# Retention and two feed-forward layers on one core: background work drawn from two queues, upper parts and rectifiers queued apart from what they depend on

## The chip, the core and the metric

The kernel runs on one core of a Trainium2 chip. A core has TensorE (PE in the profile; PEld is its loading of weights), VectorE (DVE), ScalarE (ACT), GpSimd (POOL) and SyncE (SP), each with its own queue that it works through in order, and 16 DMA engines that they share. Here nearly all DMAs are issued from SP's queue. The metric is the time of one execution in device microseconds (us).

## What is computed

```python
# retention, per batch and head, for t in 0..767 (4 batches, 8 heads, head size 64)
state = gamma * state + outer(k[t], v[t])
y[t] = scale * (q[t] @ state)
# y as x: 3072 tokens x 512, then two feed-forward layers, 512 -> 2048 -> 512
h = x @ w_in;   x = maximum(0.01 * h, h) @ w_out
h = x @ w2_in;  out = (h - tanh(h)) @ w2_out
```

Weights come as 64-bit floats and are turned into 32-bit ones on the chip.

## The kernel before

**Stages.** Retention runs first, in 24 steps of one chunk of 128 times and one pair of heads, for all batches. In step `s` TensorE transposes k of step `s+1` and a part of q, computes y of step `s` (after VectorE has put the decay on its scores: the two `A`), the state's update (`u`, not in the last chunk) and the scores of step `s+1`. ScalarE scales k (two instructions of 128x256), copies the transposes (`kT`, `qT`) and y out of PSUM. Then comes the first layer's first matrix product ("the stream" below): blocks of 128x512 by a Strassen-Winograd scheme, 3 superblocks of tokens (`sb`, two chunks of 512 tokens each) times 8 groups of weights (`g`) times 7 products (P1, P2, P5, P6, P3, P7, P4), 168 products of 6 matmuls. Last are the first layer's second product (lines 628 to 654, 96 rounds of 12 matmuls) and the second layer (96 rounds of 24).

**Split precision.** Every operand of a matmul is cut into an upper part (ScalarE rounds it, `xch`, `wgh`, `gh`) and a lower part (VectorE takes the upper part from the source, `xcl`, `wgl`, `gl`), and three matmuls take the place of one. `split` writes both, one behind the other (line 129).

**Order of the stream.** `stream` sorts the products by slot: 56 slots for each superblock, 7 for each group, and an offset from `PROD`: P1 at 0, P2 at 1, P5 at 2, P6 at 4, P3 at 5, P7 at 10, P4 at 13. PSUM banks are X (four, for P1, P6, P7, P4, which add up in one bank), Y (two, P5 and P3 in one bank) and Z (two, P2). After a product `collect` takes its bank: P1, P6 and P5 are copied out by ScalarE (`copy_out`, L563, the tile P); after P2, P3 and P7 VectorE adds a kept copy (`add_up`, L569, the tile c) and ScalarE rectifies that sum at once (`rectify`, L545), and SP stores it to `g1s`; P4 is rectified straight from its bank. P3 may start when the copy of P5 has left bank Y, P6 when the copy of P1 has left X, and P4 when VectorE has read P7's sum from X.

**Background work.** Generators issue the work that prepares operands, and each yields the VectorE time that it has just issued: `conversion` loads a raw block (512 KB), ScalarE takes its absolute value (`s1`, L159), VectorE makes the float in four instructions (`s2`, L163 to L171); `build_wg` makes the operands of a weight group from two converted blocks (sums `s12` and `s34` by VectorE, then `split`); `build_xc` makes those of a superblock of tokens (differences by VectorE, L293, and `split`); `keep_out` splits a converted `w_out` block; `store2` stores a block for the second layer. In the retention two queues run: `conv` from step 4 with 1.3 us a step, `bg` from step 8 with 1.0 us. In the stream there is one queue, `bg`, with 1.3 us a product less 0.7 where VectorE adds; its members run one after the other, and a load is waited for where the next instruction needs it.

**Code names.** The lines that the change and the prediction touch: 118 (`run`), 129, 175, 204, 222, 260, 271, 501 to 518 (retention's loop), 566, 590 to 615 (the stream's loop), 625, 748 to 778.

## Time and profile before

| | us |
|---|---|
| median of 3 runs (1199.52 to 1203.79) | 1202.17 |
| the profiled execution | 1197.38 |
| its span, first to last instruction | 1195.5 |
| retention, up to 118.80 | 118.8 |
| the stream, up to the first matmul of the second product | 286.1 |
| the rest | 790.6 |

In the rows below a line of the timeline begins with its start and its length in us from the span's start; a bracket at its end holds the time that the engine stood idle just before it and what ended that. A line of waits has who waited for whom, the us in total, the number of times and the longest. A group of instructions has its count, then busy us and mean ns of one. The granted clock is a share of full speed; in the rows by stage the DMA columns are the busy share and GB/s.

### The profile page before, as it was taken

Reading aid. Unit: us, or ns where it says so; the run is one execution under the profiler, and the core shown is the slowest. Engines: PE = TensorE matmul, PEld = TensorE weight load, DVE = VectorE, ACT = ScalarE, POOL = GpSimd, SP = SyncE. Lnnn points to the kernel's source line nnn. Section 1 sums busy time; section 2 is a strip of 40 time slices with the busy share of each in tenths; the row PEclk is TensorE's granted clock in tenths of the full one; section 3 lists DMA queues with packets and bytes.
Section 4 is the critical chain, followed back from the end, with each engine's and each line's share of the span. In section 5 each row is a group of like instructions: output and inputs, shape, how many; then the busy total and the mean of one; then the engine's idle time right before and its main releaser. Section 6 shows DMA issues by size and latency. Waiting matters only on the chain.

```text
span 1195.5 us, 16441 instructions
## 1 busy us (share of the span) xinstructions
PE 1146.0 (96%) x6075; PEld 938.3 (78%) x6075; DVE 754.5 (63%) x1264; ACT 592.9 (50%) x1025; POOL 168.6 (14%) x156
## 2 busy tenths in 40 slices
PE   9899888799899699999999999999999999999998
PEld 6788666587677588888888888888888888888886
DVE  3588674682677556544344567776767676767665
ACT  5666554554555424324444454545554544554544
POOL 2231000000000000000000132232232232232221
PEclk9999999999899899999999999999999999999999
DMA  9993464484456668645564100100200100200000
GB/s 230 266 241 92 174 223 141 147 293 177 158 194 211 234 232 311 236 155 214 211 244 136 71 1 1 71 1 1 71 1 2 71 1 1 71 1 1 36 1 36
DMA packets 134448, 148.02 MB, mean 124 GB/s; under 512 B 57440, under 2 KB 86240, under 8 KB 134368
## 3 DMA queue, kind: packets, MB, share of 16 engines
q1 hardware_dynamic: 134080, 146.83, 36.8%
q8 instruction: 47, 0.77, 0.3%
q14 instruction: 33, 0.27, 0.1%
q10 hardware_dynamic: 288, 0.15, 0.0%
HBM read 96.61 MB, written 50.33 MB: 123 GB/s over the span
## 4 chain that ended last, share of the span: by engine, by line
PE 66%; DVE 1%; DMA 0%; issue 0%; ACT 0%; SPq 0%; ACTq 0%
PE o L645 22%; PE acc L711 22%; PE h L697 22%; DVE c L569 0%; DMA gr<-g1s 0%; DMA g1s<-c 0%; DVE cv L168 0%; PE X L556 0%; ACT c L545 0%; ACT wo L132 0%; DVE cv L163 0%; DVE cv L165 0%; DVE wo L133 0%; DVE st L719 0%; ACT gh L132 0%
## 5 line engine op out<-in xcount | busy, mean ns | idle before, releaser
L133 POOL TENSOR_TENSOR gl<-e,gh 128x512 fp32r<-128x512 f32 x95 | 122.9, 1294 | 933.1 <-ACT gh L132 876.9
L645 PE MATMUL o<-gh,wo 128*128 128x512 f32 x768 | 238.5, 392 | 4.9 <-ACT gh L132 4.9
L645 PEld LDWEIGHTS o<-gh,wo 128*128 128x128 f32 x768 | 145.2, 189 | 35.6 <-ACT gh L132 5.6
L132 ACT ACTIVATE gh<-e 128x512 fp32r<-128x512 f32 x96 | 60.7, 633 | 220.2 <-DVE e L738 220.2
L731 DVE SCALAR_TENSOR_TENSOR e<-e,h 128x512 f32<-128x512 f32 x96 | 66.0, 687 | 152.4 <-ACT e L729 152.4
L645 PE MATMUL o<-gl,wo 128*128 128x512 f32 x384 | 150.4, 392 | 0.0
L711 PE MATMUL acc<-w2h,gl 128*128 128x512 f32 x384 | 149.7, 390 | 0.0
L711 PE MATMUL acc<-w2l,gh 128*128 128x512 f32 x384 | 149.5, 389 | 0.0
L711 PE MATMUL acc<-w2h,gh 128*128 128x512 f32 x384 | 149.5, 389 | 0.0
L697 PE MATMUL h<-xkl,w2h 128*128 128x512 f32 x384 | 149.5, 389 | 0.0
L697 PE MATMUL h<-xkh,w2l 128*128 128x512 f32 x384 | 149.5, 389 | 0.0
L697 PE MATMUL h<-xkh,w2h 128*128 128x512 f32 x384 | 149.5, 389 | 0.0
L133 DVE TENSOR_TENSOR gl<-gr,gh 128x512 fp32r<-128x512 f32 x96 | 65.7, 689 | 115.5 <-ACT gh L132 94.7
L132 ACT ACTIVATE gh<-gr 128x512 fp32r<-128x512 f32 x96 | 59.2, 627 | 74.1 <-DMA gr<-g1s 47.7
L545 ACT ACTIVATE c<-c 128x512 f32<-128x512 f32 x72 | 45.5, 632 | 100.9 <-DVE c L569 91.9
L645 PEld LDWEIGHTS o<-gl,wo 128*128 128x128 f32 x384 | 72.6, 189 | 15.6 <-DVE gl L133 0.4
L711 PEld LDWEIGHTS acc<-w2h,gl 128*128 128x128 f32 x384 | 72.1, 188 | 15.7 <-DVE gl L133 0.4
L711 PEld LDWEIGHTS acc<-w2h,gh 128*128 128x128 f32 x384 | 72.1, 188 | 15.0 <-ACT gh L132 0.2
L697 PEld LDWEIGHTS h<-xkh,w2h 128*128 128x128 f32 x384 | 72.1, 188 | 15.0
L697 PEld LDWEIGHTS h<-xkl,w2h 128*128 128x128 f32 x384 | 72.1, 188 | 14.9
L697 PEld LDWEIGHTS h<-xkh,w2l 128*128 128x128 f32 x384 | 72.1, 188 | 14.9
L711 PEld LDWEIGHTS acc<-w2l,gh 128*128 128x128 f32 x384 | 72.1, 188 | 14.9
(99 smaller groups left out, 2002.9 us busy)
## 6 DMA issues: line engine op xcount, KB each, us to landing
g1s<-c SPq DMA_DIRECT2D x96, 256.0 KB, 2.1
gr<-g1s SPq DMA_DIRECT2D x96, 256.0 KB, 5.5
raw<-in_moe_w_in_dram SPq DMA_DIRECT2D x32, 512.0 KB, 5.5
raw<-in_moe_w_out_dram SPq DMA_DIRECT2D x32, 512.0 KB, 4.7
w2s<-cv SPq DMA_DIRECT2D x32, 256.0 KB, 3.4
w2r<-w2s SPq DMA_DIRECT2D x16, 512.0 KB, 5.3
q<-in_q_dram SPq DMA_DIRECT2D x24, 256.0 KB, 4.0
k<-in_k_dram SPq DMA_DIRECT2D x48, 128.0 KB, 3.8
```

The source lines that it names most:

```text
L132: nc.scalar.activation(out=hi, in_=src, func=AF.Copy)
L133: eng.tensor_tensor(out=lo, in0=src, in1=hi.bitcast(F32), op=ALU.subtract)
L545: nc.scalar.activation(out=t, in_=src, func=AF.Prelu, alpha=0.01)
L645: nc.tensor.matmul(ACC[j], a, b, start=m == 0 and i == 0, stop=m == NM - 1 and i == 2)
L697: nc.tensor.matmul(h, a, b, start=kt == 0 and i == 0, stop=kt == NK - 1 and i == 2)
L711: nc.tensor.matmul(ACC[j], a, b, start=m == 0 and i == 0, stop=m == NM - 1 and i == 2)
L731: nc.vector.scalar_tensor_tensor(out=w, in0=u, scalar=C3, in1=h, op0=ALU.mult, op1=ALU.mult)
```

## The change

What it does, part by part:

- **Two queues, one allowance.** `run` takes several queues in order and goes on to the next where one yields None. Retention's loop draws from `conv` and `bg` in turn (odd steps `conv` first, even steps `bg` first), 2.3 us a step from step 5; in the stream the order is `bg`, `bx` (tokens), `conv`.
- **Loads are passed over.** A counter `tick` rises by 3 in a retention step, 1 in a stream slot, 2 in a round of the second product. A conversion's `s1` is issued 5 ticks after its load at the earliest, and the operands loaded for a superblock too.
- **Upper parts apart.** `build_wg` and `build_xc` issue upper parts ahead of the sums or lower parts of the item before. In `build_xc` the differences for T3 and T4 go to GpSimd.
- **Late rectifiers.** `add_up` notes its rectifier in `late`; the loop issues it after the next product's `collect`.
- **Moves.** The whole of `conv_in` is in retention's queue, `w2` blocks ahead of the second product are 8, not 10; the first 5 loads of `gr` are issued in the stream's last 8 slots; `split_g(n + 2)` stands behind `mm_out1(n)`; the second layer's weights may start at round 56, not 64.

```diff
-ATT_UNITS, CONV_FROM, CONV_US = 10, 4, 1.3
-BG_FROM, BG_US = 8, 1.0
+CONV_FROM, ATT_US = 5, 2.3
+LOAD_LEAD = 5
...
-    def run(queue, us):
-        while us > 0 and queue:
-            cost = next(queue[0], "end")
+    def run(queues, us):
+        while us > 0:
+            for queue in queues:
+                cost = next(queue[0], "end") if queue else None
+                if cost is not None:
+                    break
+            if cost is None:
+                return 0.0
...
+        def load(n):
+            if n < last:
+                units[n].load()
+                at[n] = tick[0] + LOAD_LEAD
...
             if n < last:
+                while tick[0] < at[n]:
+                    yield None
                 units[n].s1()
             if 1 <= n <= last:
                 yield from units[n - 1].s2()
+                load(n - 1 + ahead)
...
     def build_wg(g):
...
+        upper(ts[0], a)
         nc.vector.tensor_tensor(out=s12[:, :H2], in0=b[:, :H2], in1=b[:, H2:], op=ALU.add)
-        yield 0.37
+        yield 0.4
         nc.vector.tensor_tensor(out=s12[:, H2:], in0=s12[:, :H2], in1=a[:, :H2], op=ALU.subtract)
-        yield 0.37
...
-        yield pair(a, "A11", "A12")
-        yield pair(s12, "S1", "S2")
+        yield 0.4
+        upper(ts[2], s12)
+        lower(ts[0], ts[1], a)
+        yield 0.7
...
+        upper(ts[4], s34)
+        lower(ts[2], ts[3], s12)
+        yield 0.7
+        upper(w["N22"][0], b[:, H2:], -1.0)
+        lower(ts[4], ts[5], s34)
+        yield 0.7
+        lower(*w["N22"], b[:, H2:], -1.0)
...
     def load_xq(sb, at):
-        while now[0] < at:
+        while now[0] < at or raws[0]:
             yield None
...
+        todo = (("B11", b11, "P1", None), ("B21", b21, "P2", (nc.vector, b11, b12, b11)), ("T1", b11, "P5", None),
+                ("T2", b11, "P6", None), ("B22", b22, "P3", (nc.gpsimd, b12, b22, b12)), ("T3", b12, "P7", None),
+                ("T4", b21, "P4", None))
+        for nm, src, by, nxt in todo[:3] if part == 0 else todo[3:]:
...
+            if nm == "T2":
+                minus(nc.vector, b11, b22, b11)
+            out = [(alloc("xch", F32R), alloc("xcl", F32R)) for _ in range(2)]
             for kt in range(2):
...
+                upper(out[kt][0], src[kt])
+            yield 0.0
+            for kt in range(2):
+                lower(*out[kt], src[kt])
                 yield 0.7
...
+            if nxt:
+                minus(*nxt)
+                yield 1.3 if nxt[0] is nc.vector else 0.0
+            if nm == "T3":
+                minus(nc.gpsimd, b21, b11, b21)
...
+            tick[0] += 3
             if s >= CONV_FROM:
-                c_us = run(conv, c_us + CONV_US)
-            if s >= BG_FROM and s < len(steps) - 1:
-                b_us = run(bg, b_us + BG_US)
+                us = run((conv, bg) if s % 2 else (bg, conv), min(us + ATT_US, ATT_US))
...
-        rectify(sb, g, half_m, half_t, t, t)
+        late.append((sb, g, half_m, half_t, t, t))
...
+        done, late[:] = late[:], []
         used = collect(sb, g, nm)
+        for args in done:
+            rectify(*args)
...
-        if i >= BG_START:
-            us = run(bg, min(us + SLOT_US - used, 2.0))
+        us = run((bg, bx, conv), min(us + SLOT_US - used, SLOT_US))
+        if len(stream) - 8 <= i < len(stream) - 8 + G_AHEAD:
+            load_g(i - len(stream) + 8)
```

Where the instructions stand, at three places. In the names, `x1` is a block of y, `xch` an upper part of a token operand, `cv` a converted block, `wgh` (of the change: `wg`) a part of a weight operand, `c` a sum to be rectified.

**Retention, steps 19 and 20, ScalarE.** Before, from k's scaling in step 19 on:

```order
L382 ACTIVATE k_21_1413<-k_21_1413,lead_65 128x4x64 [waits DMAHW6_49]
L382 ACTIVATE k_21_1413<-k_21_1413,lead_65 128x4x64 [waits DMAHW7_49]
L405 ACTIVATE kT_20_1570<-kTp_20_1565 128x512 [waits PE_49,Activation_49]
L418 ACTIVATE qT_20_1497<-qTp_20_2_1572 128x2x2x128 [waits PE_49]
L464 ACTIVATE x1_50_1595<-y_19_1578 128x512 [waits PE_49]
L132 ACTIVATE xch_51_1613<-x1_2_280 128x512 [waits DVE_49]
L132 ACTIVATE xch_53_1617<-x1_4_409 128x512 [waits DVE_49]
L382 ACTIVATE k_22_1482<-k_22_1482,lead_65 128x4x64 [waits DMAHW4_49]
```

In the change, ScalarE in step 20 and the start of step 21:

```order
L498 ACTIVATE x1_59_1654<-y_20_1637 128x512 [waits PE_49]
L142 ACTIVATE xch_60_1683<-x1_1_201 128x512 [waits DVE_49]
L142 ACTIVATE xch_62_1685<-x1_3_337 128x512 [waits DVE_49]
L142 ACTIVATE xch_64_1691<-x1_6_538 128x512
L142 ACTIVATE xch_66_1693<-x1_8_673 128x512
L416 ACTIVATE k_23_1554<-k_23_1554,lead_65 128x4x64 [waits DMAHW6_49]
L416 ACTIVATE k_23_1554<-k_23_1554,lead_65 128x4x64 [waits DMAHW7_49]
L439 ACTIVATE kT_22_1705<-kTp_22_1700 128x512 [waits PE_49,Activation_49]
L452 ACTIVATE qT_22_1630<-qTp_22_2_1707 128x2x2x128 [waits PE_49]
```

And VectorE at that place in the change: the scores of step 21, then the background of step 20, then the scores of step 22:

```order
L476 SCALAR_TENSOR_TENSOR A_21_0_1676<-sc_21_0_1666,cst_100 128x512 [waits PE_49]
L476 SCALAR_TENSOR_TENSOR A_21_1_1678<-sc_21_1_1667,cst_100 128x512 [waits PE_49]
L150 SCALAR_TENSOR_TENSOR wg_53_1407<-cv_28_1016,wg_53_1407 128x256 [waits Activation_49]
L313 TENSOR_TENSOR x1_1_201<-x1_6_538,x1_1_201 128x512
L313 TENSOR_TENSOR x1_3_337<-x1_8_673,x1_3_337 128x512
L148 TENSOR_TENSOR xcl_61_1684<-x1_1_201,xch_60_1683 128x512 [waits Activation_49]
L148 TENSOR_TENSOR xcl_63_1686<-x1_3_337,xch_62_1685 128x512 [waits Activation_49]
L148 TENSOR_TENSOR xcl_65_1692<-x1_6_538,xch_64_1691 128x512 [waits Activation_49]
L476 SCALAR_TENSOR_TENSOR A_22_0_1742<-sc_22_0_1732,cst_100 128x512 [waits PE_49]
```

In the change the first two upper parts wait for differences that stand on VectorE behind step 21's scores and in the same step; before, the differences that the two upper parts of step 19 read (L293) were VectorE's work of steps 17 and 18, ahead of step 20's scores. In the change k's scaling and `kT` of step 22 stand behind four upper parts.

**The stream, third and fourth group of the first superblock, ScalarE.** Before, from P1's copy of the fourth group to P6's:

```order
L563 ACTIVATE P1_129_2143<-X_0_3_2136 128x512 [waits PE_49]
L159 ACTIVATE cv_130_2147<-raw_6_0_2115 128x512 [waits DMAHW7_49,DMAHW0_49]
L545 ACTIVATE c_131_2158<-c_131_2158 128x512 [waits DVE_49]
L563 ACTIVATE P5_132_2170<-Y_0_3_2163 128x512 [waits PE_49]
L159 ACTIVATE cv_133_2175<-raw_14_0_2119 128x512 [waits DMAHW1_49,DMAHW0_49]
L545 ACTIVATE c_134_2184<-c_134_2184 128x512 [waits DMAHW2_49,DVE_49,Activation_49]
L563 ACTIVATE P6_135_2195<-X_0_3_2136 128x512 [waits PE_49]
```

In the change, the same:

```order
L606 ACTIVATE P1_129_2140<-X_0_3_2133 128x512 [waits PE_49]
L176 ACTIVATE cv_130_2145<-raw_6_0_2045 128x512 [waits DMAHW1_49]
L606 ACTIVATE P5_132_2166<-Y_0_3_2159 128x512 [waits PE_49,Activation_49]
L588 ACTIVATE c_131_2156<-c_131_2156 128x512 [waits DMAHW0_49,DVE_49]
L142 ACTIVATE wg_135_2175<-cv_111_2029 128x512 [waits DMAHW3_49]
L606 ACTIVATE P6_143_2199<-X_0_3_2133 128x512 [waits DMAHW0_49,PE_49]
L588 ACTIVATE c_142_2190<-c_142_2190 128x512 [waits DMAHW6_49,DVE_49]
```

The rectifier of the sum after P2 (`c_131` in both) stood ahead of P5's copy and now stands behind it, and the one after P7 behind P6's copy.

**The end of the stream, SP.** Before, the stream's last three stores and the first loads for the second product (`gr`):

```order
L546 DMA g1s_69<-c_418_4032 128x512 [waits DMAHW3_49,Activation_49]
L546 DMA g1s_69<-c_419_4044 128x512 [waits DMAHW4_49,Activation_49]
L546 DMA g1s_69<-c_420_4055 128x512 [waits DMAHW5_49,Activation_49]
L628 DMA gr_423_4062<-g1s_69 128x512 [waits DMAHW6_49,PE_49]
L628 DMA gr_424_4064<-g1s_69 128x512 [waits DMAHW7_49,PE_49]
L628 DMA gr_425_4066<-g1s_69 128x512 [waits DMAHW0_49,PE_49]
```

In the change:

```order
L568 DMA gr_407_3960<-g1s_69 128x512 [waits DMAHW6_49,PE_49]
L589 DMA g1s_69<-c_404_3952 128x512 [waits DMAHW7_49,Activation_49]
L568 DMA gr_409_3972<-g1s_69 128x512 [waits DMAHW0_49,PE_49]
L568 DMA gr_412_3986<-g1s_69 128x512 [waits DMAHW1_49]
L589 DMA g1s_69<-c_413_3994 128x512 [waits DMAHW2_49,Activation_49]
L589 DMA g1s_69<-c_410_3980 128x512 [waits DMAHW3_49,Activation_49]
L170 DMA raw_15_1_4009<-in_moe_w_out_dram 128x1024 [waits DMAHW4_49,DVE_49]
```

The first five loads of `gr` stood behind the stream's last store and now stand ahead of the last four stores.

## Rows read from the trace of the kernel before

**Rows 1.** By stage: length, busy PE, PEld, DVE, ACT, POOL, granted clock, DMA:

```profile
0.00:118.80 118.80, 113.04 (x1611) 95.21 (x1611) 77.10 (x133) 72.97 (x144) 29.93 (x51) 1.00 0.81 209
118.80:404.89 286.09, 246.44 (x1009) 193.00 (x1008) 181.60 (x324) 153.39 (x278) 0.00 (x0) 0.95 0.53 187
404.89:1195.50 790.61, 786.50 (x3456) 650.11 (x3456) 495.80 (x809) 366.51 (x603) 138.69 (x105) 1.00 0.25 88
```

**Rows 2.** The chain that ended last, a piece of the second product (two rounds):

```profile
663.15 5.44 PE o L645 x24
```

**Rows 3.** What TensorE waited for between 100 and 440 us:

```profile
PE Y L556 <- ACT P L563: 21.7, 12, 4.3
PE X L556 <- DVE c L569: 7.5, 9, 2.5
PE X L556 <- ACT P L563: 2.9, 1, 2.9
PE X L556 <- ACT wgh L132: 2.5, 2, 1.3
```

**Rows 4.** What ScalarE waited for, 110 to 440 us:

```profile
ACT c L545 <- DVE c L569: 91.9, 61, 5.1
ACT cv L159 <- DMA raw<-in_moe_w_in_dram: 11.1, 5, 4.3
```

**Rows 5.** Timeline of the stream at the first superblock's end:

```profile
208.97 0.69 DVE L569 TENSOR_TENSOR c<-Z,P 128x512 f32<-128x512 f32 x1 [3.49 <-DMA g1s<-c]
209.74 0.63 ACT L545 ACTIVATE c<-c 128x512 f32<-128x512 f32 x1 [5.08 <-DVE c L569]
210.80 0.58 ACT L563 ACTIVATE P<-Y 128x512 f32<-128x512 f32 x1
211.43 0.79 PE L556 MATMUL Y<-xch,wgh 128*128 128x512 f32 x1 [3.05 <-ACT P L563]
```

**Rows 6.** Timeline where a conversion meets a load that is not there:

```profile
322.43 0.66 ACT L159 ACTIVATE cv<-raw 128x512 f32<-128x512 f32 x1 [2.89 <-DMA raw<-in_moe_w_out_dram]
325.40 0.79 PE L556 MATMUL Y<-xch,wgh 128*128 128x512 f32 x1 [3.62 <-ACT P L563]
```

**Rows 7.** Timeline at the stream's end:

```profile
398.04 0.50 PE L556 MATMUL X<-xch,wgn 128*128 128x512 f32 x1 [2.49 <-DVE c L569]
404.89 0.79 PE L645 MATMUL o<-gh,wo 128*128 128x512 f32 x1 [4.86 <-ACT gh L132]
```

**Rows 8.** Timeline of retention, steps 4 and 5:

```profile
35.63 0.66 ACT L159 ACTIVATE cv<-raw 128x512 f32<-128x512 f32 x1 [3.94 <-DMA raw<-in_moe_w_in_dram]
38.94 1.23 PE L438 MATMUL sc<-qT,kT 64*128 64x128 f32 x16 [3.07 <-ACT kT L405]
```

**Rows 9.** Timeline of retention between the scores of two steps (84.65 and 89.27):

```profile
84.65 1.16 PE L438 MATMUL sc<-qT,kT 64*128 64x128 f32 x16
85.84 1.29 DVE L442 SCALAR_TENSOR_TENSOR A<-sc,cst 128x512 f32<-128x512 f32 x2 [0.59 <-PE sc L438]
85.88 0.90 ACT L382 ACTIVATE k<-k,lead 128x256 f32<-128x256 f32 x2
86.68 0.58 ACT L405 ACTIVATE kT<-kTp 128x512 f32<-128x512 f32 x1
87.05 0.42 DVE L163 TENSOR_SCALAR cv<-cv 128x512 f32<-128x512 f32 x1
89.27 1.16 PE L438 MATMUL sc<-qT,kT 64*128 64x128 f32 x16
```

**Rows 10.** Timeline of retention's last chunk, scores of two steps that follow each other:

```profile
111.00 1.16 PE L438 MATMUL sc<-qT,kT 64*128 64x128 f32 x16
115.19 1.16 PE L438 MATMUL sc<-qT,kT 64*128 64x128 f32 x16
```

**Rows 11.** Timeline of retention with GpSimd at work beside VectorE:

```profile
87.61 3.41 POOL L394 TENSOR_TENSOR qp<-q,lead 128x256 f32<-128x256 f32 x4 [5.40 <-DMA q<-in_q_dram]
87.96 0.98 DVE L168 SCALAR_TENSOR_TENSOR cv<-raw,cv 128x512 int32<-128x512 int32 x1
```

More of the change, by code (lines that the diff above doesn't have):

```diff
@@ L173, in s2, with conversion @@
             yield 0.75
-    def conversion(units, ahead=RAW_BUFS - 1):
+    def conversion(units, ready=None, ahead=RAW_BUFS - 1):
+        while ready and not ready():
+            yield None
         last = len(units)
-        for u in units[:ahead]:
-            u.load()
+        at = {}
+        raws[0] += 1
+        def load(n):
+            if n < last:
+                units[n].load()
+                at[n] = tick[0] + LOAD_LEAD
+        for n in range(ahead):
+            load(n)
         for n in range(last + 2):
             if n >= 2:
-                cost = units[n - 2].done(units[n - 2])
-                if cost:
-                    yield cost
-            if 0 < n < last and n - 1 + ahead < last:
-                units[n - 1 + ahead].load()
+                yield from units[n - 2].done(units[n - 2])
             if n < last:
+                while tick[0] < at[n]:
+                    yield None
                 units[n].s1()
@@ L205, in keep_out @@
         WO[u.m] = alloc("wo", F32R), alloc("wo", F32R)
-        split(*WO[u.m], u.y, nc.vector)
+        nc.scalar.activation(out=WO[u.m][0], in_=u.y, func=AF.Copy)
+        yield 0.0
+        lower(*WO[u.m], u.y)
         give(u.y)
-        return 0.7
+        yield 0.7
     conv_out = [Convert(moe_w_in, moe_w_out, m, 1, keep_out) for m in range(NM)]
@@ L222, in build_wg @@
     def build_wg(g):
-        while g + NG not in UN or g not in UN:
+        while g + NG not in UN or g not in UN or len(free) < 10:
             yield None
@@ L267, in load_xq, with build_xc @@
             q[nm] = [t[:, 0], t[:, 1]]
+        arrive = tick[0] + LOAD_LEAD
+        yield 0.0
+        while tick[0] < arrive:
+            yield None
         XQ[sb] = q
-        yield 0.01
-    def build_xc(sb, done=None):
+    def build_xc(sb, part, done=None):
         while sb not in XQ:
@@ L542, in get_bank @@
         return BK[sb, g, b], False
+    late = []
     def rectify(sb, g, half_m, half_t, src, t):
@@ L588, in collect, with made @@
         return 0.0
-    bg.extend(conv)
-    bg.extend(build_wg(g) for g in (2, 3, 4))
-    bg.append(conversion(conv_in[ATT_UNITS:]))
-    bg.extend(build_wg(g) for g in range(ATT_UNITS // 2, NG))
-    bg.extend((load_xq(1, 44), build_xc(1), conversion(conv2[:W2_EARLY]), load_xq(2, SPAN + 44), build_xc(2),
-               conversion(conv_out)))
+    def made(sb):
+        return lambda: len(XC.get(sb, ())) == 7
+    conv.extend((conversion(conv2[:W2_EARLY], made(1)),
+                 conversion(conv_out, made(2))))
+    bg.extend(build_wg(g) for g in range(2, NG))
+    bx = deque()
+    for sb in range(1, NSB):
+        bx.extend((load_xq(sb, SPAN * (sb - 1) + 38), build_xc(sb, 0), build_xc(sb, 1)))
     xleft = [(c, p) for c in range(2, NC) for p in range(NPAIR)]
@@ L600 @@
         while g not in WG or bn not in XC.get(sb, {}):
-            now[0] = at_
-            if not bg or run(bg, 0.01) == 0.0:
-                raise RuntimeError(f"{sb} {g} {nm} is not ready")
+            tick[0] += 1
+            run((bg, bx, conv), 0.01)
         product(sb, g, nm)
         now[0] = at_
+        tick[0] += 1
+        done, late[:] = late[:], []
         used = collect(sb, g, nm)
+        for args in done:
+            rectify(*args)
         if sb == NSB - 1 and nm == "P4":
@@ L746, in el_2 @@
         give(gt)
[L748 to L749 removed]
     for n in range(2):
         split_g(n, nc.vector)
[L752 to L753 removed]
+    conv.append(conversion(conv2[W2_EARLY:]))
+    bg = deque([second_weights()])
     us = 0.0
+    first_x = None
     for n in range(NT):
         load_g(n + G_AHEAD)
+        while n % NM not in WO:
+            tick[0] += 1
+            run((conv,), 0.01)
+        mm_out1(n)
         split_g(n + 2, nc.vector)
[L758 to L760 removed]
+        tick[0] += 2
         nb, m = divmod(n, NM)
[L762 to L763 removed]
+        if conv:
+            us = run((conv,), min(us + (W2_US if n >= NM else 1.9), 1.9))
         else:
[L765 removed]
+            if first_x is None:
                 load_x(0)
[L767 to L770 removed]
+                first_x = n
+            if first_x + 3 <= n < first_x + 7:
+                split_x(0, n - first_x - 3, nc.vector)
+            if n >= max(first_x + 7, 3 * NM + 8):
+                us = run((bg,), min(us + 1.3, 1.4))
         k = n - (NT - 4)
@@ L774 @@
             el_1(k // 2)
-    assert not bg
-    while bg2:
-        run(bg2, 1.0)
+    assert not conv
+    while bg:
+        run((bg,), 1.0)
     for n in range(-LAG, NT):
```

113 lines of the change are left out of this document (44 added, 69 removed).

## The prediction

> **What bounds the kernel now.** I read the table by stage first [rows 1]. In the last 790.6 us TensorE is busy for 786.5 at a granted clock of 1.00, its full 2.4 GHz, and two rounds of 12 matmuls take 5.44 us [rows 2], 0.227 us a matmul. The reader is to see that nothing is left there: 3456 matmuls by 0.227 are 783.5 us. In retention TensorE is busy for 113.0 of 118.8 us with small matmuls. The stream is the loose stage: 1008 matmuls by 0.227 are 228.5 us (1.36 us a product, a "slot"), and it took 286.1, so 57.6 us are lost. The second view is what TensorE waited for [rows 3]: 21.7 us for ScalarE's copy before bank Y is used again, 2.9 for the same copy before bank X, 7.5 for VectorE's sum, 2.5 for upper parts of weights, and 4.9 at the end of the stage for the first upper part of the second product [rows 7]. That is 39.5 us of idle time. The other 18.1 are TensorE at work but slow: the granted clock was 0.95 over the stage [rows 1], and it fell from 2.4 GHz towards 1.2 behind the longer gaps.
>
> The third view says why ScalarE's copy is late. ScalarE stood 91.9 us, 61 times, in front of a rectifier whose sum VectorE had not made [rows 4]. One such place in order [rows 5]: VectorE's sum starts at 208.97, the rectifier comes at 209.74 after 5.08 us of idle ScalarE, the copy of bank Y behind it at 210.80, and TensorE starts at 211.43 after 3.05 idle. The copy itself needed only TensorE; it stood in the wrong place in the queue. A second cause has the same look from TensorE: a conversion's absolute value stands in ScalarE's queue until its block has landed (11.1 us for one of the two matrices, at longest 4.3, [rows 4]), and the copy behind it is late: 2.89 idle on ScalarE, then 3.62 on TensorE [rows 6].
>
> **The change part by part: the stream.** Late rectifiers put a rectifier behind the next product's copy, by which time TensorE's next 1.36 us have passed and the sum is normally there. Passing over loads gives a block 5 slots, 6.8 us by 1.36, more than the longest wait of 4.3 [rows 4]. Upper parts issued ahead let VectorE find them ready. By waits [rows 3], what is late next and what stays:
> - Copy before Y, 21.7 us: P3 follows P5 by two slots less its own copy, so the copy may be 2.7 us late. At the two changes of superblock it stands behind four upper parts of about 0.6 each, two of which wait for differences; I leave 0.7 us at each, about 1.5.
> - Copy before X, 2.9: nothing stays. Upper parts of weights, 2.5: 0.3 stays, since the first group is made during retention.
> - VectorE's sum, 7.5 in 9 waits, the last of them 2.49 [rows 7]. P4 follows P7 directly at the very end, where VectorE has four conversion instructions (two of 0.42 [rows 9], two of 0.69, about 2.2) between P3's sum and P7's, while two products pass: about 1.0 stays there, and half of the other 5.0: 3.5.
> - The end, 4.9. The loads of `gr` no longer stand behind the last stores, so their landing is hidden by the last products. What is late next is ScalarE: behind the last product stand P4's rectifier (0.58, like the copy [rows 5]), the late one (0.63 [rows 5]), an absolute value (0.66 [rows 6]) and the first upper part (0.6): 2.4 stays.
>
> So 7.7 us of idle stay of 39.5. The slow work goes with the gaps: 18.1 by 7.7 / 39.5 is 3.5. The stream falls from 57.6 us lost to 11.2, a gain of **46.4**. The bounds: nothing lost at all would be 57.6; if half of the loss stays, 28.8.
>
> **Retention.** The first conversion now waits two steps for its load instead of blocking ScalarE in step 4. That block held ScalarE for 3.94 us and TensorE for 3.07 [rows 8]: gain **3.1**.
>
> The alternation costs something in return. In step s the background stands behind the step's scores on VectorE: of the two `A`, started at 85.84, the next instruction begins at 87.05 [rows 9]. Before, an upper part that needed a difference was issued a step later. Now it stands in the same step (the first of the places shown with the diff), and behind it in ScalarE's queue are k's scaling and `kT`, without which TensorE can't make the next scores. Scaling starts at 85.88, `kT` ends at 87.26, the scores start at 89.27 [rows 9]: 2.0 us to spare, so scaling may start by 87.9. By the order six even steps hold such a wait. With 1.29 us for two VectorE instructions of 128x512 and 0.42 for one of half the width or with one operand [rows 9], and 0.6 for an upper part, scaling starts at
> - step 10, two differences, the second upper part: 87.05 + 1.29 + 0.05 + 0.5 = 88.9, late by 1.0;
> - step 12, a lower part and two half-wide sums: late by 1.2;
> - step 14, two half-wide sums, then an upper part and a half-wide one: 0.9;
> - steps 16 and 18, three and two half-wide ones: 1.0 and 0.9, and 0.46 more each, since in the last chunk the next scores come after 4.19 us instead of 4.62 [rows 9, 10]: 1.4 and 1.4;
> - step 20, a half-wide one, two differences and then four upper parts: 90.4, so 2.5 + 0.46 = 3.0.
>
> Together **8.9** us, all on the path, because TensorE has no slack in this stage. It can be 0 if ScalarE's and VectorE's queues run further ahead than in these rows, or some 15 if each also slows the step behind it. Net cost of retention: 5.8. The extra 0.8 us of allowance a step has cover: VectorE is busy for 77.1 of 118.8 [rows 1].
>
> **GpSimd.** Twelve differences go from VectorE to GpSimd, 12 by 0.65 (half of 1.29 [rows 9]), 7.7 us off VectorE. I cost them at nothing, since VectorE is busy for 181.6 of 286.1 in the stream [rows 1] and TensorE bounds it. But the two engines disturb each other: while GpSimd scaled q for 3.41 us, VectorE's instruction of 128x512 took 0.98 us [rows 11] and not 0.69 [rows 5]. At 0.3 for each difference it is 3.6 us of VectorE time, below what is saved. The Trainium skill (SBUF — State Buffer, "SBUF: two separate sides") is harder on this edit: GpSimd and a VectorE instruction with two SBUF inputs take a shared pair of ports as an exclusive lock, and the loser waits for the whole instruction. By it a difference of about 1.7 us (two of the four in 3.41) could hold VectorE as long, 12 by 1.7 or 20 us, more than the edit saves; the row shows a delay but no full block, and the sum goes by the row.
>
> **Rest.** The second product's first 16 rounds get 1.9 us of background each, with one lower part of 0.69: 2.6 of 2.72 [rows 2], covered as long as TensorE takes 2.72 a round. No change there.
>
> **The sum.** 46.4 + 3.1 - 8.9 = 40.6. Against the profiled execution: 1197.4 - 40.6 = 1156.8. The median of the runs lies 4.8 above that execution, so I forecast 1202.2 - 40.6 = **1161** us (chance 0.55).
>
> **The rivals.**
> - Retention doesn't pay: ScalarE's queue has more slack than the rows say. For it: it is idle for 46 of 118.8 us [rows 1]. Against it: a single late instruction there cost 3.07 [rows 8]. Then 46.4 + 3.1: 1153. Chance 0.2.
> - The change doesn't do what it says about loads: SP works in order, and a load issued behind a store that waits for a rectifier starts late, so that 5 slots are too few. Then the waits for blocks stay, 10.8 us of idle (2.9 [rows 3], 3.6 [rows 6] and the longest, 4.3 [rows 3]) with their share of slow work, by 57.6 / 39.5 is 15.8: 1177. If GpSimd's differences also hold VectorE at the superblocks' changes, up to 1185. Chance 0.17.
> - Slower: the wait that takes the rectifier's place. By the order 29 upper parts in the stream stand behind VectorE's work. If each costs TensorE what it costs in retention, 8.9 / 6 or 1.5 us, that is 43 us idle and with the slow work 63: 1161 + 63 = 1224. It turns the sign from 0.96 us each (40.6 / 29 / 1.46). Against it: in the stream the copy has 2.7 us to spare, in retention the step has 2.0, and TensorE waited only 2.5 us for such parts before [rows 3]. Chance 0.05.
> - Gains and costs within 0.3% of each other: 0.03.
>
> **How the numbers follow.** The likeliest is the sum, 1161. From 1147 (the first rival, less half of the 11.2 us that the sum leaves to the stream) to 1185 lie the forecast, the first rival and most of the second; about 0.15 is left out. A change of 0.3% is about what a measurement of this kernel can tell from none. Faster by more than that: 0.92 (0.55 + 0.2 + 0.17); within: 0.03; slower: 0.05.
>
> **What would show it.** Right: in the profile after, the stream lasts about 240 us, ScalarE's waits for VectorE's sums fall below 15 us, TensorE's wait for the copy before Y nearly goes, the gap ahead of the second product is about 2.4, and the clock over the stream is 0.98 or more. In retention six gaps of 1 to 3 us stand before the scores, with `kT` as what ended them, and no gap at 36; retention ends near 125. Wrong: gaps before Y with a conversion's absolute value or an upper part ahead of the copy, or a last stage with TensorE idle.

## The result

| | before | after |
|---|---|---|
| median of 4 runs, us | 1201.62 (1199.52 to 1203.79) | 1158.25 (1157.96 to 1158.29) |
| the profiled execution, its span | 1197.38, 1195.5 | 1157.96, 1156.2 |
| retention, up to its last matmul | 118.8 | 127.2 |
| the stream, up to the second product | 286.1 | 238.9 |
| the rest | 790.6 | 790.1 |

The ratio is 0.9638, with a 95% interval of 0.9621 to 0.9656: 3.6% faster. The spans differ by 47.2 - 8.4 + 0.5 = 39.3 us. The stages of the changed kernel, as [rows 1]:

```profile
0.00:127.20 127.20, 115.33 (x1611) 96.62 (x1611) 79.70 (x133) 73.16 (x147) 36.21 (x55) 0.99 0.78 201
127.20:366.09 238.89, 232.12 (x1009) 189.81 (x1008) 169.44 (x291) 147.50 (x270) 12.26 (x8) 0.99 0.62 216
366.09:1156.20 790.11, 786.13 (x3456) 649.48 (x3456) 506.07 (x830) 369.95 (x609) 138.78 (x105) 1.00 0.25 90
```

The granted clock of the stream rose from 0.95 to 0.99 (1.00 is 2.4 GHz throughout; below it, a part of the stretch ran at 1.2). What TensorE waited for between 20 and 400 us (total, times, longest), which answers [rows 3]:

```profile
PE sc L472 <- ACT kT L439: 9.6, 6, 2.8
PE o L691 <- ACT gh L137: 2.3, 1, 2.3
PE Y L599 <- ACT xch L142: 2.1, 1, 2.1
PE X L599 <- DVE c L612: 1.0, 1, 1.0
PE Y L599 <- DVE xcl L148: 0.9, 2, 0.6
PE X L599 <- ACT P L606: 0.5, 1, 0.5
```

The copy before bank Y, 21.7 us in [rows 3], is not in the list any more. ScalarE's waits between 115 and 365 us show why, beside [rows 4]: in front of a rectifier it stood 3.1 us for VectorE's sum instead of 91.9, and of the other engines its copies now wait for TensorE alone.

```profile
ACT P L606 <- PE Y L599: 22.8, 16, 2.1
ACT c L588 <- DVE c L612: 3.1, 2, 1.6
ACT xch L142 <- DMA g1s<-c: 2.7, 1, 2.7
```

One place in order, as [rows 5]. The copy of bank Y waits for the product only, and the rectifier comes behind it:

```profile
195.54 0.60 ACT L606 ACTIVATE P<-Y 128x512 f32<-128x512 f32 x1 [2.07 <-PE Y L599]
196.03 0.62 ACT L588 ACTIVATE c<-c 128x512 f32<-128x512 f32 x1
```

The stream's end, as [rows 7]: the last P4 waits 0.98 us, the second product 2.32.

```profile
362.11 0.50 PE L599 MATMUL X<-xch,wg 128*128 128x512 f32 x1 [0.98 <-DVE c L612]
366.09 0.51 PE L691 MATMUL o<-gh,wo 128*128 128x512 f32 x1 [2.32 <-ACT gh L137]
```

Retention has no gap at 36 any more [rows 8], and has six new ones, behind even steps 10 to 20; the last three:

```profile
95.92 1.24 PE L472 MATMUL sc<-qT,kT 64*128 64x128 f32 x16 [2.49 <-ACT kT L439]
106.08 1.22 PE L472 MATMUL sc<-qT,kT 64*128 64x128 f32 x16 [1.22 <-ACT kT L439]
117.82 1.47 PE L472 MATMUL sc<-qT,kT 64*128 64x128 f32 x16 [2.82 <-ACT kT L439]
```

### The profile page after: what moved, and what is told of

It reads as the page before. It is cut to its first block, busy times and chain, and to the rows that moved or that the text cites. A ratio compares the mean times of both kernels' runs of the same rounds, so it can differ in the third digit from the quotient of the medians.

```text
span 1156.2 us, 16460 instructions
## 1 busy us (share of the span) xinstructions
PE 1133.6 (98%) x6075; PEld 935.9 (81%) x6075; DVE 755.2 (65%) x1252; ACT 590.6 (51%) x1025; POOL 187.2 (16%) x168
## 3 DMA queue, kind: packets, MB, share of 16 engines
q1 hardware_dynamic: 134080, 146.83, 38.1%
## 4 chain that ended last, share of the span: by engine, by line
PE 79%; DVE 1%; ACT 1%; issue 1%; DMA 0%; SPq 0%; DVEq 0%; ACTq 0%
PE o L691 23%; PE acc L757 23%; PE h L743 23%; PE X L599 6%; PE Y L599 3%; PE Z L599 2%; DVE xcl L148 0%; ACT xch L142 0%; ACT c L588 0%; DMA raw<-in_moe_w_out_dram 0%; DVE c L612 0%; DVE xq_B L313 0%; ACT cv L176 0%; ACT P L606 0%; DVE cv L185 0%
## 5 line engine op out<-in xcount | busy, mean ns | idle before, releaser
L691 PEld LDWEIGHTS o<-gh,wo 128*128 128x128 f32 x768 | 144.9, 189 | 32.8 <-ACT gh L137 2.8
L599 PE MATMUL X<-xch,wg 128*128 128x512 f32 x384 | 127.7, 392 | 1.5 <-DVE c L612 1.0
L599 PEld LDWEIGHTS X<-xch,wg 128*128 128x128 f32 x384 | 72.7, 189 | 17.8 <-DVE c L612 1.6
L757 PEld LDWEIGHTS acc<-w2h,gl 128*128 128x128 f32 x384 | 72.0, 188 | 15.7 <-DVE gl L138 0.4
```

Of the source, the lines that this page charges most:

```text
L599: nc.tensor.matmul(ps, w[:, c], x, start=first and kt == 0 and i == 0, stop=kt == 1 and i == 2, skip_group_check=True)
L691: nc.tensor.matmul(ACC[j], a, b, start=m == 0 and i == 0, stop=m == NM - 1 and i == 2)
L757: nc.tensor.matmul(ACC[j], a, b, start=m == 0 and i == 0, stop=m == NM - 1 and i == 2)
```

## The experiments

Each run has the median of 4 and its ratio to runs of the kernel before that were taken beside it (medians 1199.88 to 1201.62), with the interval. Retention and stream are read from one profiled execution each. "Stream" is from the first product's first matmul to the second product's: 284.9 us before (it counts the 1.2 us ahead of the first product to retention) and 238.9 in the changed kernel. Retention has the same order of instructions in the changed kernel and in rect_now, one_queue and loads_after_stream, and took 127.2, 128.2, 124.8 and 126.0 us: read differences there under 3 us with care.

| | us | ratio (95%) | retention | stream |
|---|---|---|---|---|
| the changed kernel | 1158.25 | 0.9638 (0.9621 to 0.9656) | 127.2 | 238.9 |
| rect_now | 1170.70 | 0.9754 (0.9740 to 0.9769) | 128.2 | 250.4 |
| joined | 1155.80 | 0.9635 (0.9612 to 0.9658) | 122.3 | 241.9 |
| rect_now_joined | 1176.33 | 0.9801 (0.9783 to 0.9820) | 123.6 | 261.4 |
| lead_0 | 1179.33 | 0.9830 (0.9814 to 0.9846) | 138.2 | 248.5 |
| one_queue | 1163.54 | 0.9691 (0.9675 to 0.9708) | 124.8 | 245.2 |
| loads_after_stream | 1160.27 | 0.9666 (0.9648 to 0.9685) | 126.0 | 242.0 |
| differences_on_vector | 1155.18 | 0.9618 (0.9597 to 0.9639) | 127.2 | 237.7 |
| before_late | 1177.33 | 0.9809 (0.9786 to 0.9831) | 121.9 | 264.6 |
| before_late_lead | 1172.46 | 0.9770 (0.9751 to 0.9789) | 117.2 | 263.1 |
| later_step | 1148.81 | 0.9564 (0.9546 to 0.9581) | 118.9 | 240.8 |
| later_step_end | 1143.33 | 0.9525 (0.9503 to 0.9546) | 115.9 | 237.9 |
| best | 1139.92 | 0.9495 (0.9480 to 0.9509) | 115.4 | 234.3 |

**Late rectifiers: undone (rect_now), and alone (before_late).**

```diff
-        late.append((sb, g, half_m, half_t, t, t))
+        rectify(sb, g, half_m, half_t, t, t)
```

> The changed kernel with one part undone: a sum's rectifier is queued at once again, ahead of the next copy. Theory (the late rectifier is what frees ScalarE for the copies): TensorE waits again for the copy before bank Y, 21.7 us in the kernel before, with its share of slow work (57.6 / 39.5) 31.7, so the stream takes about 270 us instead of 238.9 and the kernel about 1158.3 + 31.7 = 1190 us. Rival (the gain is that of the two queues and of the loads that are passed over; upper parts issued ahead let VectorE make the sums early enough): the sums are no longer late, ScalarE's waits for them stay below 30 us and the kernel takes 1158 to 1166 us.

> The kernel before with one part of the change alone: a sum's rectifier is queued behind the next product's copy. Theory: the wait before bank Y (21.7 us) goes but for the places behind a late load (3.6 of it), which makes 18.1 x 1.46 = 26 us: 1201.6 - 26 = about 1175 us. Rival (the queues and loads make the gain): the waits move to the upper parts and loads that stand behind VectorE's work, and at most 8 us are gained: 1193 us or more.

On the kernel before, late rectifiers alone gain 20 us of stream, close to the theory (1177.3 us for 1175). TensorE's wait for the copy before Y falls from 21.7 to 8.1 us and not to 3.6: of the gaps left, two (2.02 and 1.76) stand where the copy is queued behind a conversion's block, and two (2.98 and 1.12) at the superblocks' changes, where it is queued behind the upper part of a token operand that itself waits for a DMA (5.11 and 3.53 us on ScalarE; the profile names a store of a sum to `g1s`). Undone in the changed kernel, the part costs 11.5 us of stream, between theory and rival, though ScalarE stands in front of the rectifiers nearly as long as in the kernel before (88.0 us against 91.9). ScalarE's and TensorE's waits of rect_now:

```profile
ACT c L588 <- DVE c L612: 88.0, 68, 3.4
PE Y L599 <- ACT P L606: 5.4, 3, 2.1
```

So what an engine waits says little about what TensorE waits: the longest wait fell from 5.1 to 3.4, and with it the copies that came too late, from 12 to 3. Something else in the change keeps VectorE's sums early; the next two runs look for it.

**Upper parts: undone (joined), and together with the rectifier (rect_now_joined).**

```diff
-                upper(out[kt][0], src[kt])
-            yield 0.0
-            for kt in range(2):
-                lower(*out[kt], src[kt])
+                upper(out[kt][0], src[kt])
+                lower(*out[kt], src[kt])
```

(and the same in `build_wg`.)

> The changed kernel with the upper parts queued again directly ahead of their own lower parts, as in the kernel before (each pair of them one behind the other, behind the sums or differences that the pair reads); late rectifiers, two queues and the passing over of loads stay. Theory: in the stream a lower part then waits on VectorE for an upper part that ScalarE has just begun, so VectorE's sums come later and TensorE waits for them (7.5 us in the kernel before, 1.0 in the changed one) and for the operands at a superblock's change (3.0 us): the stream takes 246 to 252 us instead of 238.9, and the kernel 1165 to 1172 us. Rival: with the late rectifiers neither engine is near its limit in the stream (VectorE busy 169 of 239 us), and upper parts ahead change nothing there: stream within 3 us, kernel 1155 to 1161 us.

> The changed kernel with both parts undone that part ScalarE from VectorE in the stream: a sum's rectifier is queued at once, and upper parts stand directly ahead of their own lower parts. Apart, the stream lost 11.5 us by the first (250.4 against 238.9) and 3.0 by the second (241.9). Theory (the rectifier that waits for VectorE and the lower part that waits for ScalarE are two halves of one loop, in which each engine stands in the queue behind work of the other; one half undone leaves little of it, which is why late rectifiers gave 20 us on the kernel before and lose only 11.5 here): together they lose much more than 14.5 us, the stream takes 262 to 278 us, ScalarE's waits for sums exceed 90 us, and with retention near 122 us the kernel takes 1176 to 1192 us. Rival (they add up, and the rest is of the smaller allowance of a slot and of loads): stream 252 to 256 us, kernel 1165 to 1170 us.

By itself the part is worth 3.0 us in the stream, as the rival had it, and costs 4.9 in retention, so the kernel without it is no slower. With both undone the stream takes 261.4, 8.0 more than the two losses together, a hair under the range that the theory gave, and ScalarE's waits for the sums are longer and reach TensorE again, and not in front of bank Y alone:

```profile
ACT c L586 <- DVE c L610: 95.0, 66, 4.5
PE Y L597 <- ACT P L604: 7.9, 6, 2.2
PE X L597 <- DVE c L610: 7.2, 7, 2.0
```

VectorE's waits for upper parts of tokens, weights and `w_out` (125 to 380 us) tell the same: 26.5 us in the changed kernel, 32.8 in joined, 38.1 in rect_now, 51.1 in rect_now_joined. So the loop is there: a rectifier that waits for VectorE delays an upper part, and the lower part behind that delays the next sum. One turn of it in rect_now_joined: the rectifier waits 2.27 us for a sum, behind it ScalarE copies Y (TensorE stands idle for 1.73) and makes an upper part, and VectorE waits 1.37 us for that:

```profile
149.91 0.63 ACT L586 ACTIVATE c<-c 128x512 f32<-128x512 f32 x1 [2.27 <-DVE c L610]
150.92 0.62 ACT L142 ACTIVATE wg<-cv 128x512 fp32r<-128x512 f32 x1
151.58 0.69 DVE L148 TENSOR_TENSOR wg<-cv,wg 128x512 fp32r<-128x512 f32 x1 [1.37 <-ACT wg L142]
```

Of the 22.5 us that both halves give, late rectifiers alone give 19.5 (261.4 to 241.9) and upper parts alone 11.0 (to 250.4). The loop is smaller than I had put it.

**Loads passed over (lead_0), and late rectifiers with loads on the kernel before (before_late_lead).**

```diff
-LOAD_LEAD = 5
+LOAD_LEAD = 0
```

> The changed kernel with the delay of 5 ticks between a load and its first use set to 0, so that no load is passed over. Theory: a conversion's absolute value stands in ScalarE's queue until its block has landed; 10.8 us idle in the kernel before (2.9, 3.6 and 4.3), with slow work 15.8, and the 3.1 us of retention's step 4 in part: 1170 to 1177 us. Rival: three blocks are in flight and a block takes 2.4 us of VectorE time to convert, so that a load has some 7 us anyway; then nothing shows beyond the first block of each run of conversions, and the kernel stays within 4 us of 1158.

> The kernel before with two parts of the change: late rectifiers, and a conversion's absolute value queued 5 ticks after its load at the earliest (there is still one queue in the stream, so that the work behind a load that is not there waits with it). Theory (late rectifiers and loads make nearly all of the gain, each for its own waits): from the 1177.3 of late rectifiers alone go the waits that stood behind a load: 8.1 us before bank Y, 2.0 before X, with their share of slow work by 1.46 some 15, and most of the 4.3 us in retention's step 4: about 1159 us. Rival (passing over needs a second queue to pass to: a queue that stands still makes operands late): TensorE waits for weights or for the second layer's first operands instead, and the kernel takes 1172 us or more.

Undone, this costs more than any other single part: in the stream (138 to 387 us here) ScalarE waits 13.3 and 4.8 us for blocks, at longest 4.1, and TensorE waits for a copy in the wake of that. The stream loses 9.6 us and retention 11.0, more than the 3.1 of one step that I had put there: TensorE's gaps before the scores make 6.1 us more (15.7 for 9.6, with one of 4.20 behind step 4's block), and behind them the granted clock is 0.91 from 40 to 60 us and from 80 us on, where the changed kernel has 1.00 up to its last gap.

```profile
ACT cv L176 <- DMA raw<-in_moe_w_out_dram: 13.3, 6, 4.1
ACT cv L176 <- DMA raw<-in_moe_w_in_dram: 4.8, 3, 3.2
```

One of TensorE's gaps in its timeline:

```profile
232.16 0.79 PE L599 MATMUL Y<-xch,wg 128*128 128x512 f32 x1 [3.15 <-ACT P L606]
```

Added to late rectifiers on the kernel before, the same delay gains 4.7 us in retention and 1.5 in the stream: its rival was right. With one queue nothing behind the waiting member is issued, and weights are late instead (2.28 and 2.99 us idle, in the order of the rows below). The wait before Y is 5.4 us still: both its gaps, 3.66 and 1.79, stand at the superblocks' changes behind that other wait for a DMA, which this delay doesn't touch. In the changed kernel it is still there (2.7 us in the list of ScalarE's waits), with no gap of TensorE behind it.

```profile
168.97 0.50 PE L570 MATMUL X<-xch,wgh 128*128 128x512 f32 x1 [2.28 <-ACT wgh L134]
172.68 0.80 PE L570 MATMUL X<-xch,wgl 128*128 128x512 f32 x1 [2.99 <-DVE wgl L135]
```

**One queue in the stream (one_queue).**

```diff
-        us = run((bg, bx, conv), min(us + SLOT_US - used, SLOT_US))
+        us = run((bg,), min(us + SLOT_US - used, SLOT_US))
```

> The changed kernel with one queue in the stream, as in the kernel before: weights of groups 2 and 3, the rest of the first conversion, weights of the other groups, then the tokens of each superblock and a conversion behind each; nothing is passed to when the member in front waits for a load or for a group's blocks. Late rectifiers, the delay of 5 ticks and the upper parts stay. Theory (the second and third queue are what is left of the stream's gain, 24 us between before_late_lead, 263.1 us, and the changed kernel, 238.9): with one queue VectorE's slots are lost while the member in front waits, operands come late, and the stream takes 250 us or more, the kernel 1170 us or more. Rival (that gain is of the other parts: all blocks' conversion begun in retention, loads for the second product ahead of the last stores): within 3 us of 1158.3.

The stream is 6.3 us longer, less than the theory asked and more than the rival: one gap of 6.64 and one of 2.03 us where a group's weights stand behind the conversion, but no gap at the superblocks' changes.

```profile
PE X L599 <- ACT wg L142: 6.6, 1, 6.6
PE X L599 <- DVE wg L148: 2.0, 1, 2.0
```

**Loads for the second product behind the stream (loads_after_stream).** The five `load_g` calls stand behind the last product.

> The changed kernel with the first five loads of the second product (gr) issued behind the stream's last product, as in the kernel before. Theory of the prediction (their landing ends the wait of 4.9 us at the stream's end, and ScalarE's queue alone leaves 2.3): the gap ahead of the second product grows from 2.3 to 5 to 7 us, and the kernel takes 1161 to 1165 us, by some 2 us more if TensorE runs slow behind the longer gap. Rival (ScalarE's queue is the whole of the gap): 1157 to 1159.5 us.

The gap is 5.11 us instead of 2.32, as the prediction had it (ScalarE stood 2.67 us before the first upper part, waiting for its load), and the last stage is 0.7 us longer (790.8). The median is 2.0 us more, 0.7 below the range, and its interval overlaps that of the changed kernel, so what is shown is the gap and not the time.

```profile
368.03 0.79 PE L689 MATMUL o<-gh,wo 128*128 128x512 f32 x1 [5.11 <-ACT gh L137]
```

**The differences (differences_on_vector).**

```diff
-("B22", b22, "P3", (nc.gpsimd, b12, b22, b12))
+("B22", b22, "P3", (nc.vector, b12, b22, b12))
...
-                minus(nc.gpsimd, b21, b11, b21)
+                minus(nc.vector, b21, b11, b21)
```

> The changed kernel with the twelve differences of T3 and T4 on VectorE again and not on GpSimd. Theory of the prediction (they cost nothing on either engine): within 2 us of 1158. Rival A (GpSimd's work slows VectorE's work beside it by more than the edit saves, as the Trainium skill, SBUF — State Buffer, states): the gaps of 2.1 and 0.9 us at the superblocks' changes shrink and the kernel takes 1154 to 1156 us. Rival B (VectorE's 7.7 us more are on the path at the superblocks' changes): 1160 to 1166 us.

The stream is 1.2 us shorter, and the gap for the first upper part at the superblock's change falls from 2.11 to 0.53 us. The interval of the time overlaps that of the changed kernel, so GpSimd's work gains nothing here. The profiled spans differ by 2.9 us, of which 1.6 lie in the last stage, where none of these differences stands. There the second product begins behind the same gap of 2.32 us, yet its first 10 us run at a granted clock of 1.00 (2.4 GHz) with 42 matmuls; in the changed kernel it was 0.83 with 35:

```profile
364.83 0.51 PE L692 MATMUL o<-gh,wo 128*128 128x512 f32 x1 [2.32 <-ACT gh L137]
364.83:374.83 10.00, 9.78 (x42) 1.00 0.86 290
```

So the same gap is not always followed by slow matmuls. Of the five profiles with this gap of 2.32 us (the changed kernel, joined, one_queue, later_step and this one) four show 0.83 behind it and this one 1.00.

**The order in retention (later_step).**

```diff
+    def later():
+        t = tick[0]
+        while att[0] and tick[0] <= t:
+            hold[0] = True
+            yield None
+        hold[0] = False
...
+        yield from later()
         upper(ts[2], s12)
...
-                us = run((conv, bg) if s % 2 else (bg, conv), min(us + ATT_US, ATT_US))
+                us = run((conv, bg) if s % 2 and not hold[0] else (bg, conv), min(us + ATT_US, ATT_US))
```

(`later()` stands ahead of the upper parts of `s34`, T1, T2, T3 and T4 too, and T2's difference now counts as 1.3 us of allowance; `att` is True in retention.)

> The changed kernel, where in retention an upper part that reads a sum or difference of VectorE is issued one step after it (eight such places; a queue that waits for that is drawn first in the next step). Theory (the order of those upper parts makes the six gaps): the gaps before the scores, 9.6 us in the changed kernel and about 1.8 us of slow matmuls behind the last of them, go; retention ends near 116 instead of 127.2, and the kernel takes 1147 to 1149 us. Rival (VectorE has more work in a step than the step has room for, with 2.3 us of allowance and GpSimd's scaling beside it): the gaps stay, with the scores waiting for VectorE's or ScalarE's later work, and the kernel stays within 3 us of 1158.

All six gaps are gone. What stands in this profile is one gap of another kind, 1.94 us behind VectorE's state update; in the next two kernels, with the same rule in retention, it is 0.88 us behind a copy of `qT` and none, and retention takes 115.9 and 115.4. The rival falls: the same work fits into the steps once its order is changed. The kernel takes 1148.8 us, in the range, though retention as profiled is 118.9 and not 116.

```profile
98.67 1.85 PE L504 MATMUL y<-qT,U 64*64 64x128 f32 x16 [1.94 <-DVE U L529]
```

**The end of the stream (later_step_end), and all that helped (best).**

```diff
         used = collect(sb, g, nm)
+        if i >= len(stream) - 2:
+            split_g(i - len(stream) + 2, nc.vector)
         for args in done:
             rectify(*args)
...
-    for n in range(2):
-        split_g(n, nc.vector)
```

> The kernel of later_step, and the upper and lower parts for the second product's first two rounds issued in the stream's last two slots, ahead of the late rectifier and the background's absolute value. Theory (the 2.32 us gap ahead of the second product is ScalarE's queue alone): the gap falls to 0.5 us or less and the kernel takes 1.8 us less than later_step, 1146 to 1147.5. Rival (the parts' stores, loads or buffers are late, so the gap stays or moves to VectorE's last sum): 1148 to 1150.

The gap is gone entirely. The median is 5.5 us below that of later_step (4.7 by the ratios) where 1.8 were expected; later_step's four runs lie between 1145.94 and 1151.93, so the size is not sharp. The gap gives 2.3 us and the last stage another 2.3, from 790.1 to 787.8: behind the gap TensorE had been slow, in later_step as in the changed kernel, where the first 10 us of the second product have 35 matmuls at a granted clock of 0.83. Here they have 46 at 1.00. The rows of the changed kernel (length, busy PE with its matmuls, clock, DMA):

```profile
366.09:376.09 10.00, 9.78 (x35) 0.83 0.85 281
```

And in later_step_end:

```profile
353.86:363.86 10.00, 10.00 (x46) 1.00 0.92 315
```

> The kernel of later_step_end, with the differences of T3 and T4 on VectorE as in differences_on_vector, and 2.6 us of allowance in a step of retention instead of 2.3. Theory (what is left in later_step_end's stream is the chain at the first superblock's change, 3.2 us of idle at 192 to 198 and some 3 us of slow matmuls behind it, where VectorE's lower parts took 1.58 and 1.17 us beside GpSimd's differences instead of 0.65): both go for the greater part, and the kernel takes 1138 to 1141 us against 1143.3. Rival (VectorE's 7.7 us more, and the greater allowance, put work on the path in retention or at that change): 1143 us or more.

The kernel takes 1139.9 us, in the range. It differs from later_step_end in two things, the engine of the differences and the allowance, and no run tells them apart. Its stages, with the granted clock at 1.00 in all three:

```profile
0.00:115.43 115.43, 112.21 (x1612) 95.07 (x1612) 78.33 (x135) 73.98 (x147) 31.93 (x51) 1.00 0.85 217
115.43:349.72 234.29, 231.47 (x1009) 188.59 (x1009) 169.91 (x299) 147.27 (x266) 0.00 (x0) 1.00 0.63 219
349.72:1137.90 788.18, 784.16 (x3457) 648.23 (x3455) 506.72 (x831) 372.27 (x612) 138.57 (x105) 1.00 0.25 91
```

TensorE's two longest waits from 20 to 400 us are now 1.0 us for VectorE's last sum and 0.5 for an upper part of a token operand. This kernel beats both, by 5.0% the one before and by some 1.5% (18.3 us by the medians) the changed one.

## Why the prediction was right, point by point

**The stream, 46.4 us.** It gave 47.2. Of idle time 7.0 us stay (7.7 forecast) and of slow work 3.4 (3.5): 238.9 less 228.5 is 10.4. By terms: before Y no copy is waited for. Where 1.5 was put for a late copy at the superblocks' changes, 3.0 us stand at the first one for P5's own operands, an upper part (2.11) and lower parts (0.63 and 0.22). That term had the place and not the mechanism. The upper part reads a difference that VectorE ended at 203.94, but in ScalarE's queue it stands behind a late rectifier, which waited 1.53 us for a sum that VectorE made behind the differences:

```profile
202.65 1.29 DVE L313 TENSOR_TENSOR xq_B<-xq_B,xq_B 128x512 f32<-128x512 f32 x2
204.57 0.63 ACT L588 ACTIVATE c<-c 128x512 f32<-128x512 f32 x1 [1.53 <-DVE c L612]
205.11 1.14 ACT L142 ACTIVATE xch<-xq_B 128x512 fp32r<-128x512 f32 x2
```

That is the fault that the change removes elsewhere: putting the rectifier behind the next copy doesn't keep it from standing ahead of something else that TensorE needs. The copy before X leaves 0.5, not 0; weights' upper parts 0, not 0.3; the sums 1.0, all of it at the last P4, where 3.5 stood; the end 2.3 and 0.2, for 2.4.

**The reasons behind that sum were less good than the sum.** The prediction gave the 21.7 us before Y to the rectifier's place and to loads, and named the upper parts beside them without a price. By the runs the parts overlap: the rectifier is worth 20 us on the kernel before and 11.5 on the changed one; with the upper parts 22.5; the loads 9.6; the further queues 6.3; the loads ahead of the last stores 3.1; GpSimd -1.2. Added up that would be 40.3 of the 46.0 by which the stream as measured here fell; but losses of single parts undone need not add up, as the rectifier and the upper parts show, so this is no exact account, and what is left has not been told apart. That 46.4 came so close is in part luck: two of its terms were off by 1.5 and 2.5 us in opposite directions.

**Retention, a gain of 3.1 and a cost of 8.9.** The gain came. The six gaps stood where they were put, with `kT` as what ended them, and make 9.6 us: 1.17, 1.18, 0.76, 2.49, 1.22 and 2.82, where 1.0, 1.2, 0.9, 1.4, 1.4 and 3.0 were forecast. The mis-sized term is step 16, 2.49 for 1.4. There VectorE's half-wide instructions took 0.82, 0.83 and 0.72 us instead of the 0.42 of [rows 9], because GpSimd was scaling q beside them, which the step left out:

```profile
91.52 2.88 POOL L428 TENSOR_TENSOR qp<-q,lead 128x256 f32<-128x256 f32 x4 [5.75 <-PE qTp L451]
91.60 0.82 DVE L150 SCALAR_TENSOR_TENSOR wg<-cv,wg 128x256 fp32r<-128x256 f32 x1
92.34 0.83 DVE L265 TENSOR_TENSOR s<-cv 128x256 f32<-128x256 f32 x1
93.21 0.72 DVE L267 TENSOR_TENSOR s<-s,cv 128x256 f32<-128x256 f32 x1
93.96 0.63 ACT L142 ACTIVATE wg<-s 128x512 fp32r<-128x512 f32 x1 [4.00 <-DVE s L267]
```

The sum also put at nothing that the matmuls behind a gap may be slow, which the step named only in its upper bound of 15. Behind the gap of 2.82 the granted clock was 0.80 to retention's end, and 8.40 by 0.20 is some 1.7 us:

```profile
118.80:127.20 8.40, 8.40 (x106) 6.75 (x102) 6.24 (x12) 1.71 (x3) 0.00 (x0) 0.80 0.01 2
```

So retention cost 8.4 net where 5.8 stood. The clock's part of it is not fixed: the same gap of 2.82 us was followed by 1.00 in differences_on_vector and one_queue, by 0.82 and 0.80 in rect_now and loads_after_stream. Two readings in this step were off without moving the sum: the next scores come 0.43 us earlier in the last chunk (4.62 less 4.19), not 0.46, and from step 8 on the allowance is 2.3 us before and after, so there were no 0.8 us more to cover. That the price was one of order and not of VectorE's load is shown by later_step.

**GpSimd at nothing.** The runs put the loss at some 1 us of stream, not clear of noise, so the sum stood; but the reading of [rows 11], "a delay but no full block", did not (last section).

**The sum and the median.** 40.6 forecast, 39.3 measured between the profiled executions. The 4.8 us by which the median stood above the profiled execution didn't come back: the changed kernel's runs lie within 0.3 us of each other, at 1158.25 where 1161 was forecast. The sum was only 1.3 too high because its errors partly cancel: the stream gave 0.8 more, retention cost 2.6 more, and the last stage gave 0.5. The rivals: loads were not late (ScalarE waited for no block between 115 and 365 us), dependent upper parts in the stream cost 2.1 us and not 43, and retention did cost. In the argument against the third, the copy before Y has not 2.7 us to spare but some 2.1: two products pass between P5 and P3, 2.7 us, and the copy itself takes 0.6 of them.

## What to carry to other kernels

An instruction that waits for another engine belongs behind everything in its queue that another engine is already waiting for; two engines that each queue such waits at once make a loop, and here breaking one half of it gave half of the gain or more, so neither a part alone nor a part undone tells what the part is worth. The same holds for the reverse side of this change: operands prepared ahead should read what was made a step earlier, since a queue's tail (here the scaling of k and `kT`) pays for a wait of the step itself. And price a gap of TensorE with what may follow it: in the changed kernel gaps of 2.3 and 2.8 us cost another 2.3 and 1.7 in slow matmuls, while in differences_on_vector the same two gaps cost nothing more. A gap's cost is a range, and a single profile shows only one value of it.

## What the hardware showed that I had not expected

GpSimd's instructions and VectorE's with two operands in SBUF held each other up by what was left of the other's instruction. Spans on GpSimd are rough in a profile, but here they fit to 0.1 us. At the first superblock's change in later_step_end, GpSimd's two differences took 1.60 and 1.73 us, and VectorE's lower parts 1.58 and 1.17 us beside them, while a sum that reads PSUM between them took its usual 0.68. In best, with no work on GpSimd there, the same two lower parts take 1.29 together. The timeline of later_step_end:

```profile
193.38 1.60 POOL L323 TENSOR_TENSOR xq_B<-xq_B,xq_B 128x512 f32<-128x512 f32 x1 [94.29 <-DVE xq_B L323]
194.94 1.73 POOL L323 TENSOR_TENSOR xq_B<-xq_B,xq_B 128x512 f32<-128x512 f32 x1
193.94 1.58 DVE L148 TENSOR_TENSOR xcl<-xq_B,xch 128x512 fp32r<-128x512 f32 x1
195.45 0.68 DVE L634 TENSOR_TENSOR c<-Z,P 128x512 f32<-128x512 f32 x1
196.05 1.17 DVE L148 TENSOR_TENSOR xcl<-xq_B,xch 128x512 fp32r<-128x512 f32 x1
```

The same two in the timeline of best:

```profile
193.00 1.29 DVE L148 TENSOR_TENSOR xcl<-xq_B,xch 128x512 fp32r<-128x512 f32 x2
```

GpSimd's first difference ends at 193.38 + 1.60 = 194.98; the lower part beside it ends at 195.52, 0.54 us later. The second difference ends at 196.67, and the lower part beside it at 197.22, 0.55 later. A lower part of 0.65 that can do nearly nothing until the difference has ended would do just that. GpSimd pays too: where it comes first and no such work of VectorE is under way, such a difference takes 1.29 us in the same run (at 199.52), and these took 1.60 and 1.73. The Trainium skill (SBUF — State Buffer, "SBUF: two separate sides") states an exclusive lock for the whole instruction, and these rows agree with it.

[rows 11], which the prediction read as a partial delay, show the same when the four scalings are read one by one in the kernel before. They took 0.79, 1.06, 1.06 and 0.61 us, 3.41 together, where the four take 2.34 in most other steps. The first is

```profile
87.61 0.79 POOL L394 TENSOR_TENSOR qp<-q,lead 128x256 f32<-128x256 f32 x1 [5.40 <-DMA q<-in_q_dram]
```

It ended at 88.40, and VectorE's instruction, begun at 87.96, ended at 88.94, again 0.54 us later. So its 0.29 us of delay was a full wait for the rest of a short instruction, and the larger part of the price, 1.07 us, stood on GpSimd, where the prediction didn't look.
